# Pooled attention and a gated feed-forward on one core: GpSimd writes the scaled queries in tile order, and VectorE's reciprocal gives a third factor

## The chip, the core and the metric

The kernel runs on one core of a Trainium2 chip. The metric is the time of one execution on the device in microseconds (us); the median of three runs of the kernel before is 1849.12 us (1848.44 to 1851.25). One execution was also taken by the profiler, and all rows below come from it. The engines are named as in the profile: PE (TensorE's matmuls), PEld (its weight loads), DVE (VectorE), ACT (ScalarE), POOL (GpSimd), SP (the queue that issues the DMAs). L544 is line 544 of the kernel before.

## The reference

Two stages over 4 batches of 12288 tokens with 128 channels. First, attention against 768 keys that are at once the values: `kv` is averaged over 4x4 patches and multiplied by `w_sr`. Then a feed-forward of width 1024, whose activation is h times its own softmax, with a layer norm behind it.

```python
kv_pool = kv.reshape(B, H // r, r, W // r, r, C).mean(axis=(2, 4))
k = v = kv_pool.reshape(B, -1, C) @ w_sr
s = (q @ k.transpose(0, 2, 1)) / np.sqrt(C)
a = np.exp(s - s.max(-1, keepdims=True))
a /= a.sum(-1, keepdims=True) + 1e-09
x = (a @ v).reshape(B * N, C)
h = x @ w_in
e = np.exp(h - h.max(-1, keepdims=True))
solu = h * e / (e.sum(-1, keepdims=True) + 1e-9)
ln = (solu - mean(solu)) / np.sqrt(var(solu) + 1e-6) * g_ln
out = ln @ w_out
```

## The kernel before

The 49152 tokens are 384 **tiles** of 128 tokens; 4 tiles are a **group** (512 tokens, one load of queries), 24 groups are a batch. The program is written out by hand as 384 **slots**, one per tile, and every engine works its own in-order queue. In each slot each stage works on another tile: slot t does the scores of tile t+1, a quarter of the attention's values of an earlier group, the first feed-forward matmul (`hidden_pe`, L693) of tile t-9, the activation of tiles t-10 and t-11, and the last matmul (`final_pe`, L821) of tile t-13. Most matmuls are done in three passes over 16-bit halves (a high and a low part), so operands are split into a high part (a cast) and a low part (a subtraction).

What one slot holds, engine by engine:

- PE: 6 matmuls of scores (L580), 4 or 5 of values (L640), 6 of `h` (L693), 24 of the output `o` (L821).
- DVE: the row maximum of the scores (L601), the low half `phl` of the probabilities (L612), the maximum of `h` (L701), and `u` = h x factor x e (L731).
- ACT: the exponential of the scores (L602), the high half of `phl` (L604), a square for the variance (L796), the exponential `e` (L717).
- POOL: the high half of `u` (`hidden_high`, L748, 128x1024) and its low half (`hidden_low`, L755), both into the tile `uhl`.
- SP: issues two DMA transposes: `pT` from `phl` (L615), which the values need, then `uT` from `uhl` (L770), which the output matmul of that tile reads two slots later.

Once in a group come: the load of queries `qf` (L528), POOL's scaling of them (`q_scale`, L544, batches 1 to 3 only), ACT's cast to `qh` (`q_split`, L558), POOL's low part `ql` (`q_low`, L567), the norms (below), `xh` and `xl`, the output's scale `f` (L831 to L839), the output tile `ob` and its store. While a batch runs, POOL also sums the pooling patches of the next batch (`kv_add`, L240, 128x384, two in 6 slots; in batch 0 more), each sum behind a load of 384 KB on SP. In batch 0 the scores use 32-bit operands: there `q_split` and `q_low` work on `qwh` and `qwl`, and the queries are not scaled.

The queries of a group lie in `qf` as token order has them; token 4t+j belongs to row t of tile j. `by_tile` reads them with a stride of 4 elements (16 bytes), so that a result written through `in_tiles` has the 128 tokens of each tile side by side. Before the change `q_scale` works in place, in order; `q_split` and `q_low` read through `by_tile`:

```python
nc.gpsimd.tensor_scalar(qf, qf, state["kq", g // GPB][:, 1:2], 1.0, op0=ALU.mult, op1=ALU.mult)
nc.scalar.copy(in_tiles(qh), by_tile(qf))
nc.gpsimd.tensor_tensor(in_tiles(ql), by_tile(qf), in_tiles(high), op=ALU.subtract)
```

The norms of a group: `values_norm` (POOL, L667) makes two rows `zz` of 4 sums, z times `bb[3]` and z times `bb[4]`; `values_recip` (DVE, L675) inverts both into `rz`, factors for the exponential of `h` and for its maximum; `values_recip_u` (ACT, L680) multiplies the first by `bb[0]`, which is the factor of `u`. `bb` holds factors of a batch, set once by small operations (`kv_bound0`).

Within a slot POOL's queue stands as: zz (one slot in four), high and low of `u`, `f` (another slot), `q_low` (a third), `q_scale` (the slot of zz), then `kv_add`.

Of the kernel before, what the change touches and what calls it, by code (L numbers as in the profile page):

```python
# [11 lines left out]
F32 = mybir.dt.float32  # L12
# [9 lines left out]
P = 128  # L22
# [45 lines left out]
def kernel(  # L68
# [38 lines left out]
    def float64_parts(raw, name):  # L107


        pair = raw.rearrange("p (f two) -> p f two", two=2)  # L110
        lo, hi = pair[:, :, 0], pair[:, :, 1]
        top = wrk.tile([P, DFF], F32, tag="u", name=f"top_{name}", bufs=5)
        if name == "in":
            rest = wrk.tile([P, DFF], F32, tag="u", name="rest_in", bufs=5)
        else:
            rest = bat.tile([P, 2 * NK], F32, tag="acc", name="rest_out", bufs=1)[:, :DFF]
        ex = wrk.tile([P, DFF], I32, tag="e", name=f"ex_{name}")
        sgn = wrk.tile([P, DFF], I32, tag="e", name=f"sgn_{name}")
        scalar = nc.vector.tensor_scalar
        both = nc.vector.tensor_tensor  # L120
        and_, shr = ALU.bitwise_and, ALU.logical_shift_right
        return top, rest, [
            partial(scalar, ex, hi, 20, 0x7FF, op0=shr, op1=and_),
            partial(scalar, ex, ex, -896.0, 0.0, op0=ALU.add, op1=ALU.max),
            partial(scalar, ex, ex, 255.0, 2.0**23, op0=ALU.min, op1=ALU.mult),
            partial(
                nc.vector.scalar_tensor_tensor,
                ex,
                hi,
                -0x80000000,  # L130
                ex,
                op0=and_,
                op1=ALU.bitwise_or,
            ),
            partial(scalar, sgn, hi, 0xFFFFF, 3, op0=and_, op1=ALU.logical_shift_left),
            partial(both, top.bitcast(I32), ex, sgn, op=ALU.bitwise_or),
            partial(
                nc.vector.scalar_tensor_tensor,
                rest,
                lo.bitcast(U32),  # L140
                2.0**-52,
                ex.bitcast(F32),
                op0=ALU.mult,
                op1=ALU.mult,
            ),
        ]
# [4 lines left out]
    def kv_alloc(b):  # L151
        for n, w, dt, bufs in (
            ("kT", NK, F32, 1),
            ("ksq", NK, BF16, 1),
            ("kss", 2, F32, 4),
            ("vf", NK, F32, 1),
        ):
            state[n, b] = bat.tile([P, w], dt, tag=n, name=f"{n}_{b}", bufs=bufs)
        for n, w in (("knm", 3), ("sv", 2), ("bb", 5), ("kq", 3), ("dg", P)):
            state[n, b] = (  # L160
                state[n, 0]
                if 0 < b < B
                else bat.tile([P, w], F32, tag=n, name=f"{n}_{b}", bufs=1)
            )
        for n, dt, bufs in (
            (("kwh", F32R, 1), ("kwl", F32R, 1))
            if b == 0 or b >= B
            else (("kh", F16, 2), ("kl", F16, 2))
        ):
            state[n, b] = bat.tile([P, NK], dt, tag=n, name=f"{n}_{b}", bufs=bufs)  # L170
        vhl = dmt.tile([P, 2 * NKC, P], F16, tag="vhl", name=f"vhl_{b}")
        state["vhl", b] = vhl
        state["vh", b], state["vl", b] = vhl[:, :NKC, :], vhl[:, NKC:, :]
# [181 lines left out]
    def kv_bound0(part):  # L355
        knm, bb, sv = state["knm", 0], state["bb", 0], state["sv", 0]
        if part == 0:
            nc.vector.tensor_scalar(
                bb[:, 0:1], knm[:, 2:3], wmax2, 1e-20, op0=ALU.mult, op1=ALU.max
            )  # L360
            nc.vector.tensor_scalar(knm[:, 2:3], knm[:, 2:3], 1e-28, None, op0=ALU.max)
            nc.gpsimd.tensor_tensor(knm[:, 2:3], knm[:, 2:3], mhalf[:, 0:1], op=ALU.pow)
            nc.gpsimd.tensor_tensor(bb[:, 0:1], bb[:, 0:1], mhalf[:, 0:1], op=ALU.pow)
        elif part == 1:
            pow2_under(knm[:, 2:3])
        else:
            small(bb[:, 1:2], bb[:, 0:1], SC / 32 * 1e-3 * 2.0**15)
            small(bb[:, 0:1], bb[:, 0:1], SC / 32)
            small(bb[:, 2:3], bb[:, 1:2], 1e-9)
            small(bb[:, 3:4], knm[:, 2:3], 2.0**5, wsc)  # L370
            small(bb[:, 4:5], bb[:, 3:4], -1.0)
            small(sv[:, 1:2], sv[:, 1:2], knm[:, 2:3], 2.0**5 / (SC * SC))

    def kv_scale_v(b, part):
# [12 lines left out]
    def kv_bound(b, part):  # L387

        knm, bb, sv = state["knm", b], state["bb", b], state["sv", b]
        if part == 0:
            nc.vector.tensor_reduce(knm[:, 2:3], knm[:, 0:2], axis=AX.X, op=ALU.max)
            nc.vector.tensor_scalar(
                bb[:, 0:1], knm[:, 2:3], wmax2, 1e-20, op0=ALU.mult, op1=ALU.max
            )
            nc.vector.tensor_scalar(knm[:, 2:3], knm[:, 2:3], 1e-28, None, op0=ALU.max)
            nc.gpsimd.tensor_tensor(bb[:, 0:1], bb[:, 0:1], mhalf[:, 0:1], op=ALU.pow)
            nc.gpsimd.tensor_tensor(knm[:, 2:3], knm[:, 2:3], mhalf[:, 0:1], op=ALU.pow)  # L400
        elif part == 1:
            nc.vector.tensor_scalar(
                bb[:, 1:2], bb[:, 0:1], SC * 1e-3 * 2.0**15, None, op0=ALU.mult
            )
            nc.vector.tensor_scalar(bb[:, 0:1], bb[:, 0:1], SC, None, op0=ALU.mult)
            nc.vector.tensor_scalar(bb[:, 2:3], bb[:, 1:2], 1e-9, None, op0=ALU.mult)
            pow2_under(knm[:, 2:3])
        else:
            nc.vector.tensor_scalar(knm[:, 2:3], knm[:, 2:3], 2.0**5, None, op0=ALU.mult)
            nc.vector.tensor_scalar(bb[:, 3:4], knm[:, 2:3], wsc, None, op0=ALU.mult)  # L410
            nc.vector.tensor_scalar(bb[:, 4:5], bb[:, 3:4], -1.0, None, op0=ALU.mult)
            nc.vector.tensor_scalar(sv[:, 1:2], sv[:, 1:2], knm[:, 2:3], None, op0=ALU.mult)

    def kv_diag(b, half):
# [119 lines left out]
    def in_tiles(a):  # L534
        return a.rearrange("p (j t) -> p j t", j=GT)
# [4 lines left out]
    def q_scale(g):  # L540
        if wide(g) or NG <= g:
            return
        qf = state["qf", g // QL][:, (g % QL) * 512 : (g % QL + 1) * 512]
        nc.gpsimd.tensor_scalar(  # L544
            qf, qf, state["kq", g // GPB][:, 1:2], 1.0, op0=ALU.mult, op1=ALU.mult
        )

    def q_split(g):
        if NG <= g < NG + GPB:
            return  # L550
        qf = state["qf", g // QL][:, (g % QL) * 512 : (g % QL + 1) * 512]
        if wide(g):
            qh = grp.tile([P, 512], F32R, tag="qwh", name=f"qwh_{g}")
            ql = grp.tile([P, 512], F32R, tag="qwl", name=f"qwl_{g}")
        else:
            qh = grp.tile([P, 512], F16, tag="qh", name=f"qh_{g}")
            ql = grp.tile([P, 512], F16, tag="ql", name=f"ql_{g}")
        nc.scalar.copy(in_tiles(qh), by_tile(qf))  # L558
        state["q", g] = (qh, ql)

    def q_low(g):
        if NG <= g < NG + GPB:
            return
        qf = state["qf", g // QL][:, (g % QL) * 512 : (g % QL + 1) * 512]
        qh, ql = state["q", g]
        high = qh.bitcast(F32) if wide(g) else qh
        nc.gpsimd.tensor_tensor(in_tiles(ql), by_tile(qf), in_tiles(high), op=ALU.subtract)  # L567


    def scores_pe(t):  # L570
# [89 lines left out]

    def values_norm(g):
        b = g * GT // TPB
        zz = grp.tile([P, 2, GT], F32, tag="zz", name=f"zz_{g}", bufs=2)
        rz = grp.tile([P, 3, GT], F32, tag="rz", name=f"rz_{g}", bufs=3)
        z, bb = state.pop(("z", g)), state["bb", b]
        for k in range(2):
            nc.gpsimd.tensor_scalar(  # L667
                zz[:, k, :], z, 1e-9, bb[:, 3 + k : 4 + k], op0=ALU.add, op1=ALU.mult
            )
        state["zz", g] = (zz, rz)  # L670

    def values_recip(g):

        zz, rz = state.pop(("zz", g))
        nc.vector.reciprocal(rz[:, 0:2, :], zz)  # L675
        state["rz", g] = [rz[:, k, :] for k in range(3)]

    def values_recip_u(g):
        rz = state["rz", g]
        nc.scalar.activation(rz[2], rz[0], AF.Copy, scale=state["bb", g * GT // TPB][:, 0:1])  # L680
        state["z2", g] = grp.tile([P, GT], F32, tag="z2", name=f"z2_{g}", bufs=3)
        state["v3", g] = grp.tile([P, GT], F32, tag="v3", name=f"v3_{g}", bufs=3)

# [637 lines left out]
```

## Time and profile before

| | |
|---|---|
| median of 3 runs | 1849.12 us (1848.44 to 1851.25) |
| the profiled execution | 1851.55 us, of which the trace spans 1849.8 us |
| PE busy | 1821.7 us (98%) |
| ACT busy | 1783.7 us (96%) |
| DVE busy | 1769.8 us (96%) |
| POOL busy | 1683.1 us (91%) |
| granted TensorE clock | 0.999 of full speed |

The profiled execution took 2.43 us more than the median. PE's busy time is counted from matmuls that overlap, so a busy PE need not be at its peak. Busy shares are means over stages with different limits; the table says that four engines are full nearly all the time, not which of them sets the pace. SP is not in the table: the time in which it issues DMAs is not counted as busy.

### The profile page before, as it was taken

How to read it: one execution, taken by the hardware profiler on the slowest of the kernel's cores; microseconds unless marked ns; L12 is line 12 of the kernel's file. 1: busy time of each engine (PE TensorE's matmuls, PEld its weight loads, DVE VectorE, ACT ScalarE, POOL GpSimd, SP SyncE). 2: the span in 40 equal slices, each digit the busy share in tenths (PEclk: the TensorE clock that was granted, in tenths of full speed). 3: DMA queues.
4: the chain of work that ended last, by engine and by line, in shares of the span. 5: the costliest groups of instructions: out<-in, count | busy, mean ns of one | idle time of the engine just before them, and what ended most of it. 6: DMA issues, size and time to landing. Idle time of an engine off the chain costs nothing.

```text
span 1849.8 us, 42799 instructions
## 1 busy us (share of the span) xinstructions
PE 1821.7 (98%) x15747; PEld 1190.7 (64%) x15747; DVE 1769.8 (96%) x2635; ACT 1783.7 (96%) x3129; POOL 1683.1 (91%) x1466
## 2 busy tenths in 40 slices
PE   8999999999999999999999999999999999999998
PEld 5567777776566666666666666666666666666666
DVE  6999999999999999999999999999999999999997
ACT  5999999999999999999999999999999999999997
POOL 5899999899999999989999999998998989898987
PEclk9999999999999999999999999999999999999999
DMA  8999999999999999999999999999999999999998
GB/s 301 213 219 244 232 244 239 234 235 224 231 243 240 239 239 237 242 236 240 237 245 233 228 244 239 245 243 222 220 228 235 241 230 223 234 229 229 226 224 170
DMA packets 1440027, 432.80 MB, mean 234 GB/s; under 512 B 1404608, under 2 KB 1408832, under 8 KB 1439552
## 3 DMA queue, kind: packets, MB, share of 16 engines
q1 hardware_dynamic: 1439664, 429.97, 114.9%
q8 instruction: 126, 2.06, 0.5%
q14 instruction: 93, 0.76, 0.1%
q10 hardware_dynamic: 144, 0.00, 0.0%
HBM read 52.50 MB, written 25.17 MB: 42 GB/s over the span
## 4 chain that ended last, share of the span: by engine, by line
PE 66%; POOL 14%; ACT 9%; DMA 4%; issue 4%; DVE 2%; POOLq 0%; DVEq 0%
PE o L821 19%; PE h L693 18%; PE s L580 14%; PE xa L640 13%; POOL uhl L755 6%; DMA uT<-uhl 4%; POOL uhl L748 4%; ACT junk L796 2%; ACT e L717 2%; ACT s L602 2%; ACT phl L604 2%; POOL ql L567 1%; POOL ka L240 1%; PE pk L201 1%; POOL f L839 1%
## 5 line engine op out<-in xcount | busy, mean ns | idle before, releaser
L755 POOL TENSOR_TENSOR uhl<-u,uhl 128x1024 f16<-128x1024 f32 x382 | 814.5, 2133 | 31.7
L821 PEld LDWEIGHTS <-uT 128*128 128x128 f16 x9072 | 535.9, 98 | 105.3 <-DMA uT<-uhl 22.7
L821 PE MATMUL o<-wch,uT 128*128 128x128 f16 x6048 | 568.3, 219 | 10.1 <-DMA uT<-uhl 9.6
L821 PE MATMUL o<-wcl,uT 128*128 128x128 f16 x3024 | 525.9, 219 | 0.0
L731 DVE SCALAR_TENSOR_TENSOR u<-h,rz,e 128x1024 f32<-128x1024 f32 x384 | 491.1, 1279 | 26.8 <-ACT e L717 19.4
L701 DVE TENSOR_SCALAR_CACHE_REDUCE junkd<-h,rz 128x1024 bf16<-128x1024 f32 x384 | 490.8, 1278 | 1.6 <-PE h L693 1.3
L640 PE MATMUL xa<-pT,vhl 128*128 128x512 f16 x1728 | 469.5, 380 | 0.0
L748 POOL TENSOR_SCALAR uhl<-u 128x1024 f16<-128x1024 f32 x379 | 395.7, 1044 | 73.8 <-DVE u L731 65.6
L717 ACT ACTIVATE e<-h,nm,rz 128x1024 f32<-128x1024 f32 x384 | 458.6, 1194 | 3.0 <-DVE junkd L701 3.0
L796 ACT ACTIVATE junk<-u,su 128x1024 bf16<-128x1024 f32 x384 | 437.5, 1139 | 0.1
L601 DVE TENSOR_REDUCE nm<-s 128x1 f32<-128x768 f32 x384 | 364.2, 948 | 24.4 <-PE s L580 20.5
L612 DVE SCALAR_TENSOR_TENSOR phl<-s,phl 128x768 f16<-128x768 f32 x384 | 365.8, 953 | 2.9 <-ACT phl L604 2.8
L602 ACT ACTIVATE s<-s,nm 128x768 f32<-128x768 f32 x384 | 334.9, 872 | 9.7 <-DVE nm L601 9.0
L604 ACT ACTIVATE phl<-s 128x768 f16<-128x768 f32 x384 | 311.1, 810 | 12.1
L693 PEld LDWEIGHTS <-xh 128*128 128x128 f16 x1536 | 141.7, 98 | 195.0 <-DVE phl L612 33.1
L640 PEld LDWEIGHTS <-vhl 128*128 128x128 f16 x1728 | 162.7, 98 | 139.9 <-issue 12.8
L693 PE MATMUL h<-w_in_h,xh 128*128 128x512 f16 x768 | 228.9, 380 | 2.4 <-DVE rz L675 1.3
L693 PE MATMUL h<-w_in_h,xl 128*128 128x512 f16 x768 | 228.4, 379 | 0.0
L693 PE MATMUL h<-w_in_l,xh 128*128 128x512 f16 x768 | 228.4, 379 | 0.0
L580 PEld LDWEIGHTS <-qh 128*128 128x128 f16 x1152 | 107.7, 98 | 55.3 <-issue 0.7
L580 PE MATMUL s<-kh,qh 128*128 128x384 f16 x576 | 140.5, 325 | 0.6 <-DVE u L731 0.6
L580 PE MATMUL s<-kh,ql 128*128 128x384 f16 x576 | 140.7, 326 | 0.2 <-POOL ql L567 0.2
(153 smaller groups left out, 1862.7 us busy)
## 6 DMA issues: line engine op xcount, KB each, us to landing
kv<-in_kv_dram SPq DMA_DIRECT2D x64, 384.0 KB, 4.6
qf<-in_q_dram SPq DMA_DIRECT2D x96, 256.0 KB, 3.3
out_dram<-ob SPq DMA_DIRECT2D x96, 256.0 KB, 2.7
pT<-phl SPq DMA_TRANSPOSE x384, 4.0
uT<-uhl SPq DMA_TRANSPOSE x378, 4.5
raw_in<-in_moe_w_in_dram SPq DMA_DIRECT2D x1, 1024.0 KB, 5.2
raw_out<-in_moe_w_out_dram SPq DMA_DIRECT2D x1, 1024.0 KB, 9.5
room<-uhl SPq DMA_TRANSPOSE x5, 5.2
```

The lines of the kernel that those rows point to most:

```text
L580: nc.tensor.matmul(s[:, half, :384], lh[:, ts], rh[:, half * 384 : (half + 1) * 384], start=n == 0, stop=n == 2,)
L602: nc.scalar.activation(s, s, AF.Exp, bias=nm, accum_out=state["z", g][:, j : j + 1])
L612: nc.vector.scalar_tensor_tensor(phl[:, 1], state.pop(("s", t)), SC, phl[:, 0], op0=ALU.mult, op1=ALU.subtract)
L640: nc.tensor.matmul(xa, v[:, c, :], pT[:, :, a * NKC + c, :], start=n == 0, stop=n == len(seq) - 1)
L693: nc.tensor.matmul(h[:, hs], lh[:, ts], rh[:, hs], start=n == 0, stop=n == 2)
L701: nc.vector.tensor_scalar(junk, state["h", t], state["rz", g][1][:, j : j + 1], None, op0=ALU.mult, op1=ALU.min, accum_out=nm,)
L717: nc.scalar.activation(e, state["h", t], AF.Exp, bias=nm, scale=state["rz", g][0][:, js], accum_out=state["z2", g][:, js],)
L731: nc.vector.scalar_tensor_tensor(u, state.pop(("h", t)), state["rz", g][2][:, j : j + 1], state.pop(("e", t)), op0=ALU.mult, op1=ALU.mult, ...
L748: nc.gpsimd.tensor_scalar(uhl[:, 0, :], u, 1.0, 1.0, op0=ALU.mult, op1=ALU.mult)
L755: low.tensor_tensor(uhl[:, 1, :], u, uhl[:, 0, :], op=ALU.subtract)
L796: nc.scalar.activation(junk, u, AF.Square, scale=-float(DFF), bias=su, accum_out=state["v3", g][:, j : j + 1],)
L821: nc.tensor.matmul(po[:, ts], uT[:, a * NFC + c, :], w[:, c, :], start=start, stop=stop)
```

## The change

Four parts, and one that makes room:

1. `q_scale` writes a new tile `qs` (one buffer): it reads `qf` through `by_tile` and writes in tile order.
2. In batches 1 to 3 `q_split` (ACT) and `q_low` (POOL) read `qs` through `in_tiles`, that is in order. Batch 0 still reads `qf` through `by_tile`.
3. `bb` gets a sixth factor, `bb[3]` divided by `bb[0]`, set once (one DVE reciprocal, one small POOL product; the same in the general path, which does not run here).
4. `values_norm` makes a third row of `zz` from it, the reciprocal of DVE takes 12 elements in place of 8, and ACT's small product (L680) is gone, in all 96 groups.
5. `rest_out`, used while the weights are prepared, lies in the tag `uhl` in place of `acc`.

```diff
--- before.py
+++ after.py
@@ -113,7 +113,7 @@
         if name == "in":
             rest = wrk.tile([P, DFF], F32, tag="u", name="rest_in", bufs=5)
         else:
-            rest = bat.tile([P, 2 * NK], F32, tag="acc", name="rest_out", bufs=1)[:, :DFF]
+            rest = dmt.tile([P, DFF], F32, tag="uhl", name="rest_out", bufs=5)
         ex = wrk.tile([P, DFF], I32, tag="e", name=f"ex_{name}")
         sgn = wrk.tile([P, DFF], I32, tag="e", name=f"sgn_{name}")
         scalar = nc.vector.tensor_scalar
@@ -156,7 +156,7 @@
             ("vf", NK, F32, 1),
         ):
             state[n, b] = bat.tile([P, w], dt, tag=n, name=f"{n}_{b}", bufs=bufs)
-        for n, w in (("knm", 3), ("sv", 2), ("bb", 5), ("kq", 3), ("dg", P)):
+        for n, w in (("knm", 3), ("sv", 2), ("bb", 6), ("kq", 3), ("dg", P)):
             state[n, b] = (
                 state[n, 0]
                 if 0 < b < B
@@ -369,6 +369,8 @@
             small(bb[:, 2:3], bb[:, 1:2], 1e-9)
             small(bb[:, 3:4], knm[:, 2:3], 2.0**5, wsc)
             small(bb[:, 4:5], bb[:, 3:4], -1.0)
+            nc.vector.reciprocal(bb[:, 5:6], bb[:, 0:1])
+            small(bb[:, 5:6], bb[:, 5:6], bb[:, 3:4])
             small(sv[:, 1:2], sv[:, 1:2], knm[:, 2:3], 2.0**5 / (SC * SC))
 
     def kv_scale_v(b, part):
@@ -409,6 +411,8 @@
             nc.vector.tensor_scalar(knm[:, 2:3], knm[:, 2:3], 2.0**5, None, op0=ALU.mult)
             nc.vector.tensor_scalar(bb[:, 3:4], knm[:, 2:3], wsc, None, op0=ALU.mult)
             nc.vector.tensor_scalar(bb[:, 4:5], bb[:, 3:4], -1.0, None, op0=ALU.mult)
+            nc.vector.reciprocal(bb[:, 5:6], bb[:, 0:1])
+            nc.vector.tensor_scalar(bb[:, 5:6], bb[:, 5:6], bb[:, 3:4], None, op0=ALU.mult)
             nc.vector.tensor_scalar(sv[:, 1:2], sv[:, 1:2], knm[:, 2:3], None, op0=ALU.mult)
 
     def kv_diag(b, half):
@@ -541,9 +545,11 @@
         if wide(g) or NG <= g:
             return
         qf = state["qf", g // QL][:, (g % QL) * 512 : (g % QL + 1) * 512]
+        qs = grp.tile([P, 512], F32, tag="qs", name=f"qs_{g}", bufs=1)
         nc.gpsimd.tensor_scalar(
-            qf, qf, state["kq", g // GPB][:, 1:2], 1.0, op0=ALU.mult, op1=ALU.mult
-        )
+            in_tiles(qs), by_tile(qf), state["kq", g // GPB][:, 1:2], 1.0, op0=ALU.mult, op1=ALU.mult
+        )
+        state["qs", g] = qs
 
     def q_split(g):
         if NG <= g < NG + GPB:
@@ -555,7 +561,8 @@
         else:
             qh = grp.tile([P, 512], F16, tag="qh", name=f"qh_{g}")
             ql = grp.tile([P, 512], F16, tag="ql", name=f"ql_{g}")
-        nc.scalar.copy(in_tiles(qh), by_tile(qf))
+        src = by_tile(qf) if wide(g) else in_tiles(state["qs", g])
+        nc.scalar.copy(in_tiles(qh), src)
         state["q", g] = (qh, ql)
 
     def q_low(g):
@@ -564,7 +571,8 @@
         qf = state["qf", g // QL][:, (g % QL) * 512 : (g % QL + 1) * 512]
         qh, ql = state["q", g]
         high = qh.bitcast(F32) if wide(g) else qh
-        nc.gpsimd.tensor_tensor(in_tiles(ql), by_tile(qf), in_tiles(high), op=ALU.subtract)
+        src = by_tile(qf) if wide(g) else in_tiles(state.pop(("qs", g)))
+        nc.gpsimd.tensor_tensor(in_tiles(ql), src, in_tiles(high), op=ALU.subtract)
 
 
     def scores_pe(t):
@@ -660,10 +668,10 @@
 
     def values_norm(g):
         b = g * GT // TPB
-        zz = grp.tile([P, 2, GT], F32, tag="zz", name=f"zz_{g}", bufs=2)
+        zz = grp.tile([P, 3, GT], F32, tag="zz", name=f"zz_{g}", bufs=2)
         rz = grp.tile([P, 3, GT], F32, tag="rz", name=f"rz_{g}", bufs=3)
         z, bb = state.pop(("z", g)), state["bb", b]
-        for k in range(2):
+        for k in range(3):
             nc.gpsimd.tensor_scalar(
                 zz[:, k, :], z, 1e-9, bb[:, 3 + k : 4 + k], op0=ALU.add, op1=ALU.mult
             )
@@ -672,12 +680,10 @@
     def values_recip(g):
 
         zz, rz = state.pop(("zz", g))
-        nc.vector.reciprocal(rz[:, 0:2, :], zz)
+        nc.vector.reciprocal(rz, zz)
         state["rz", g] = [rz[:, k, :] for k in range(3)]
 
     def values_recip_u(g):
-        rz = state["rz", g]
-        nc.scalar.activation(rz[2], rz[0], AF.Copy, scale=state["bb", g * GT // TPB][:, 0:1])
         state["z2", g] = grp.tile([P, GT], F32, tag="z2", name=f"z2_{g}", bufs=3)
         state["v3", g] = grp.tile([P, GT], F32, tag="v3", name=f"v3_{g}", bufs=3)
```

POOL's queue in batch 1, around the scaling of one group's queries (`uhl` is the split of `u`, `zz` the sums of the norms, `qf`, `qs`, `ql` the queries), before:

```order
L544 TENSOR_SCALAR qf_11690<-qf_11690,kq_117 128x512
L667 TENSOR_SCALAR zz_12074<-z_all,bb_116 128x4 x2
L748 TENSOR_SCALAR uhl_12078<-u_12063 128x1024
L755 TENSOR_TENSOR uhl_12078<-u_12063,uhl_12078 128x1024
L748 TENSOR_SCALAR uhl_12155<-u_12145 128x1024
L755 TENSOR_TENSOR uhl_12155<-u_12145,uhl_12155 128x1024
L567 TENSOR_TENSOR ql_12138<-qf_11690,qh_12137 128x512
```

and now:

```order
L549 TENSOR_SCALAR qs_12026<-qf_11710,kq_117 128x512
L675 TENSOR_SCALAR zz_12096<-z_all,bb_116 128x4 x3
L754 TENSOR_SCALAR uhl_12101<-u_12085 128x1024
L761 TENSOR_TENSOR uhl_12101<-u_12085,uhl_12101 128x1024
L754 TENSOR_SCALAR uhl_12177<-u_12167 128x1024
L761 TENSOR_TENSOR uhl_12177<-u_12167,uhl_12177 128x1024
L575 TENSOR_TENSOR ql_12160<-qs_12026,qh_12159 128x512
```

No instruction has moved; a third small product stands behind the scaling, ahead of the next tile's split, and the scaling and the subtraction have other operands.

ACT's queue in batch 2, between the exponential of one tile and that of the next (`rz` the factors of the norms, `qh` the cast queries), before:

```order
L796 ACTIVATE junk_17342,v_57_17068<-u_17324,su_17325 128x1024
L717 ACTIVATE e_17347,z_57_17067<-h_17281,nm_231_17344,rz_17044 128x1024
L680 ACTIVATE rz_17336<-rz_17336,bb_116 128x4
L558 CAST qh_17398<-qf_16956 128x512
L602 ACTIVATE s_17328,z_all<-s_17328,nm_17401 128x2x384
```

and now:

```order
L802 ACTIVATE junk_17383,v_57_17107<-u_17364,su_17365 128x1024
L723 ACTIVATE e_17388,z_57_17106<-h_17321,nm_231_17385,rz_17083 128x1024
L565 CAST qh_17438<-qs_17306 128x512
L610 ACTIVATE s_17368,z_all<-s_17368,nm_17441 128x2x384
```

The small product is gone and the cast reads `qs`; the rest stands as it did. SP's queue has the same DMAs in the same order.

## Rows read from the trace of the kernel before

**Rows 1.** ACT's factor of u (L680), one in a group, in four stretches (first, last start)

```profile
L680 ACT ACTIVATE rz<-rz,bb x10: 287/290/292, 165.8 to 334.4; 128x4 f32<-128x4 f32 x10
...
L680 ACT ACTIVATE rz<-rz,bb x17: 282/287/290, 469.5 to 770.7; 128x4 f32<-128x4 f32 x17
...
L680 ACT ACTIVATE rz<-rz,bb x17: 282/287/290, 923.6 to 1222.1; 128x4 f32<-128x4 f32 x17
...
L680 ACT ACTIVATE rz<-rz,bb x24: 283/285/289, 1372.7 to 1795.5; 128x4 f32<-128x4 f32 x24
```

**Rows 2.** Busy us in two stretches: PE, PEld, DVE, ACT, POOL, then clock, DMA share, GB/s

```profile
461.00:777.00 316.00, 310.39 (x2726) 196.51 (x2724) 305.58 (x454) 308.07 (x538) 295.95 (x257) 1.00 1.20 239
...
1364.00:1787.00 423.00, 423.00 (x3728) 269.72 (x3727) 416.85 (x622) 420.09 (x739) 378.69 (x329) 1.00 1.16 230
```

**Rows 3.** The chain that ended last, 1139 to 1148 us: start, length, what

```profile
1133.05 6.80 DMA uT<-uhl
...
1139.90 1.51 PE o L821 x24
...
1143.25 1.29 PE h L693 x6
1144.55 1.34 PE o L821 x24
1145.89 0.97 PE s L580 x6
1146.86 1.08 PE xa L640 x5
```

**Rows 4.** Timeline of SP in batch 2, around 1130 us: start, length, what

```profile
1128.89 2.54 SPq L770 DMA_TRANSPOSE uT<-uhl  x1
1131.53 1.43 SPq L615 DMA_TRANSPOSE pT<-phl  x1
1133.05 3.26 SPq L770 DMA_TRANSPOSE uT<-uhl  x1
```

**Rows 5.** Timeline of POOL at the same place

```profile
1126.38 0.61 POOL L667 TENSOR_SCALAR zz<-z_all,bb 128x4 f32<-128x4 f32 x2
...
1128.21 2.13 POOL L755 TENSOR_TENSOR uhl<-u,uhl 128x1024 f16<-128x1024 f32 x1
```

**Rows 6.** Timeline of DVE at the same place

```profile
1127.24 0.95 DVE L612 SCALAR_TENSOR_TENSOR phl<-s,phl 128x768 f16<-128x768 f32 x1
1128.11 0.19 DVE L675 RECIPROCAL rz<-zz 128x8 f32<-128x8 f32 x1
```

**Rows 7.** Timeline of SP in batch 3, around 1505 us

```profile
1504.72 0.53 SPq L853 DMA_DIRECT2D out_dram<-ob  x1
1505.93 1.40 SPq L615 DMA_TRANSPOSE pT<-phl  x1
```

**Rows 8.** POOL's waits in 150:337, 461:777 and 915:1223: us, times, longest

```profile
POOL uhl L748 <- DVE u L731: 3.7, 7, 1.2
...
POOL uhl L748 <- DVE u L731: 8.8, 12, 1.4
...
POOL uhl L748 <- DVE u L731: 4.9, 6, 1.3
```

**Rows 9.** The operations that change, whole trace: ns least/median/most, first and last start

```profile
L544 POOL TENSOR_SCALAR qf<-qf,kq x72: 678/687/705, 446.9 to 1773.6; 128x512 f32<-128x512 f32 x72
L558 ACT CAST qh<-qf x72: 1099/1111/1137, 450.4 to 1777.4; 128x512 f16<-128x512 f32 x72
L567 POOL TENSOR_TENSOR ql<-qf,qh x72: 1386/1406/1424, 455.9 to 1782.9; 128x512 f16<-128x512 f32 x72
```

**Rows 10.** Operations of the same forms that read in order, whole trace

```profile
L271 ACT CAST kh<-kT x6: 498/500/505, 373.8 to 1289.6; 128x384 f16<-128x384 f32 x6
L274 POOL TENSOR_TENSOR kl<-kT,kh x6: 910/912/934, 380.7 to 1295.9; 128x384 f16<-128x384 f32 x6
...
L755 POOL TENSOR_TENSOR uhl<-u,uhl x382: 2124/2132/2151, 60.8 to 1831.9; 128x1024 f16<-128x1024 f32 x191
```

## The prediction

> **What bounds the kernel now.** I read the pace first, then busy times, then the chain, then the queues.
>
> *The pace.* ACT's factor of u runs once in a group of 4 tiles, so first and last start over the count less one give a group's time [rows 1]: batch 0 (334.4 - 165.8) / 9 = 18.73 us; 461 to 777 us, in batch 1, (770.7 - 469.5) / 16 = 18.83; 915 to 1223 us, in batch 2, 298.5 / 16 = 18.66; batch 3, 422.8 / 23 = 18.38.
>
> *What PE alone needs.* Where PE runs without a hole, the pieces of the chain give the matmuls' own pace [rows 3]: 0.97 us for 6 score matmuls, 1.08 for 5 of values (0.216 each), 1.29 for 6 of h, 1.34 for 24 of o. A group has 4 x (0.97 + 1.29 + 1.34) + 18 x 0.216 = 18.29 us. Batch 3 goes at 18.38, with 423.00 us of PE in 423.00 us [rows 2]: there PE sets the pace to within 0.1 us a group. Batch 0, whose scores are of 32 bits and dearer, holds its pace as evenly. Only the two stretches in between are slower than PE needs: 18.83 - 18.38 = 0.45 us a group over 316 / 18.83 = 16.8 groups (7.5 us), and 0.28 us over 308 / 18.66 = 16.5 groups (4.6 us). That, 12 us, is about all that any relief can win in these stretches.
>
> *What is late there.* The chain shows it: a transpose uT 6.80 us from issue to landing, and PE's output matmuls starting 0.05 us behind its end, with 1.51 us for what takes 1.34 elsewhere [rows 3]. But the transpose's input was no cause. Its POOL subtraction ended at 1128.21 + 2.13 = 1130.34 [rows 5], and SP issued it at 1133.05, 2.7 us later, because SP was busy: the uT before to 1131.43, then a pT to 1132.96, each behind the last by 0.1 us [rows 4]. That pT too had lain ready: its VectorE half ended at 1127.24 + 0.95 = 1128.19 [rows 6], 3.3 us before its issue. So in the stretches with kv loads SP's queue (or the transfers that hold each issue for 1.4 to 3.3 us) runs without a hole and sets the pace; what feeds it has 2.7 to 3.3 us in hand. In batch 3, with no kv loads, SP has holes: 1504.72 + 0.53 to 1505.93 is 0.68 us [rows 7].
>
> *ACT is full, but does not set the pace.* It is busy 308.07 / 316 = 97.5% in batch 1's slow stretch and 420.09 / 423 = 99.3% in batch 3 [rows 2], where PE runs at its own pace.
>
> *POOL is the other one to look at.* It waited for u 3.7 us in 150 to 337 us (10 groups), 8.8 in 461 to 777 and 4.9 in 915 to 1223 [rows 8]: 0.37, 0.52 and 0.30 us a group. The rest is work.
>
> **The change, part by part.**
>
> *ACT.* The factor's 0.29 us per group goes [rows 1]. The cast takes 1111 ns read with stride [rows 9]; kh, in order, takes 500 ns for 384 elements [rows 10], so 512 take between 500 and 500 x 512 / 384 = 667, I take 610. Together 0.79 us a group in batches 1 to 3, some 72 x 0.5 + 96 x 0.29 = 64 us of ACT's time. On the path: nothing in the slow stretches, since what ACT feeds (phl, then pT) already waits for SP. In batch 3 at most the 18.38 - 18.29 = 0.09 us a group above PE's need, 23 groups: 2 us, if ACT causes any of it. I take 0.
>
> *DVE.* The reciprocal takes 12 elements for 8, in 0.19 us now [rows 6]; half as many again can cost no more than half of that, 0.1 us x 96 = 9 us. DVE is at 305.58 / 316 = 97% in the slow stretch [rows 2], with 0.6 us a group free: 0. Removing ACT's product shortens the way from zz to u by one step.
>
> *POOL, three terms a group.* Two zz take 0.61 us with the gap between them [rows 5]; half of that is 0.31, and a third one brings its own gap, so I take 0.34. ql, now read in order: kl takes 912 ns for 384 elements and the split of u 2132 for 1024 [rows 10], so 512 take 912 + 128 x 1220 / 640 = 1156, that is 1406 - 1156 = 0.25 us less [rows 9]. The scaling now reads with the stride and took 687 ns in order [rows 9]. No row shows that operation with a stride. Bounds: 0 (the stride hides behind its arithmetic), and 1111 - 610 = 0.50 us (what the same stride costs ACT's cast, also one input, one read per element). POOL's own stride costs the 0.25 that ql loses. I take 0.35, between the same engine and the same form. Sum: 0.34 - 0.25 + 0.35 = +0.44 us a group in batches 1 to 3 (bounds +0.09 and +0.59), +0.34 in batch 0.
>
> The row of ql, with two inputs, gives 0.25 us for the stride [rows 9, 10]. The Trainium skill (GPSIMD Engine Reference, section 7, Performance pitfalls for Q7 kernels) says that a GpSimd kernel that reads at a byte step over 8 pays about 2.9 cycles per element instead of 1.9, half as much again; by that the scaling would take 687 x 1.5 = 1.03 us, an estimate, and POOL's sum would be 0.34 us a group by the row and 0.43 by the page. No run here shows which.
>
> *What covers it.* 150 to 337 us: 10 x 0.34 = 3.4 us into 3.7 of waiting: 0. 461 to 777: 16.8 x 0.44 = 7.4 into 8.8: 0. 915 to 1223: 16.5 x 0.44 = 7.3 into 4.9: 2.4 over, and first it eats the 2.7 us that a finished uhl waits for SP [rows 4, 5]: 0 to 2.4, I take 2. Batch 3 has no sums of patches, and POOL is at 378.69 / 423 = 90% [rows 2]: 0. If the cover were gone, each further 0.1 us a group would cost 33 x 0.1 = 3 us in the two stretches.
>
> *What is late next.* zz ended at 1126.99 and its reciprocal began at 1128.11, 1.1 us later [rows 5, 6]. The scaling ahead of it (+0.35) and the third product (+0.34) take 0.7 of that. A wait of DVE for zz should show in some groups, and cost little while SP is behind.
>
> *Small things.* Two operations on one column, once; rest_out in another buffer, no transfer: 0. SP's queue keeps its DMAs and order.
>
> Sum: +2 us on 1851.55, so 1853.6 for an execution like the profiled one; that stood 2.43 us above the median, so 1851 for the median.
>
> **The rivals.**
>
> *No change to measure (the forecast).* SP and its transfers keep the pace, PE in batches 0 and 3; POOL's work goes into its waits. A measurement tells 0.2% from no change, 3.7 us. Time 1851, 1847 to 1853.
>
> *Slower: POOL becomes the bound.* Its work a group is 18.66 - 0.30 = 18.36 us in batch 2's stretch and 18.83 - 0.52 = 18.31 in batch 1's. From +0.30 (batch 2) and +0.52 (batch 1) on, POOL is slower than SP's pace and uT waits for uhl instead of for SP. At the upper bound of +0.59: 16.5 x 0.29 + 16.8 x 0.07 = 6 us; and if half of POOL's present waits (7 us of 13.7) stay as they are, because u comes late behind each stall of PE, up to 13 us. Middle +7: 1856, up to 1862. For it: POOL's margin is as thin as the addition. Against: the 2.7 us that uhl lies ready.
>
> *Faster: ACT was in the loop.* If SP's holes come from late phl after all, 0.79 us of free ACT per group takes away half of the 12 us: 1843. For it: ACT is at 97 to 99%. Against: pT lay ready 3.3 us before its issue. A page bears on it: the Trainium skill (DMA: Bandwidth & Descriptors, Latency and other measured facts) gives 261 GB/s for a DMA transpose; the core moves 239 in the slow stretch [rows 2], so by the page the transfers have 8% to spare and would not bind, and PE would after any relief. The trace's SP queue without holes speaks against that.
>
> *The change doesn't do what it says.* The cast keeps its 1.11 us because its form, not the stride, is dear. Then ACT wins 0.29 us a group only and the time is the forecast's.
>
> **How the numbers follow.** No change 0.50 (with the last rival), slower 0.34, faster 0.16. The predicted time is the likeliest case's, 1851 us. The range leaves out the far half of the faster case (0.08) and the far third of the slower one (0.11): 1844 to 1859; the likeliest case's own range is 1847 to 1853.
>
> **What would show it.** Right: the cast at 0.6 us, ql at 1.16, the scaling near 1.03, three zz; ACT's share down by 4 points and POOL's up by 2; groups at 18.73, 18.8, 18.7 and 18.38 as before; SP still without holes until 1223 us. Wrong: uT issued within 0.1 us of the end of its uhl in batches 1 and 2, and groups at 18.9 or more (POOL binds), or groups near 18.4 there (ACT was in the loop).

## The result, and the profile after

The changed kernel takes 1865.20 us (median of 4 runs, 1864.67 to 1866.23), the kernel before 1848.78 beside it (4 runs, 1847.02 to 1851.25): a ratio of 1.0089 [1.0071, 1.0106]. It is slower by 16.4 us. The forecast was 1851, its range ended at 1859. The profiled execution took 1864.67 us, 13.1 more than the profiled one before. Two executions far outside all others, 10017.04 us of the kernel before and 4425.62 us of e6, are left out of the ratios and of e6's median.

The head of the page of the changed kernel, and its chain of work by engine:

```profile
span 1862.8 us, 42801 instructions
...
PE 1830.4 (98%) x15747; PEld 1190.3 (64%) x15747; DVE 1776.0 (95%) x2636; ACT 1734.9 (93%) x3033; POOL 1727.6 (93%) x1563
...
POOL 41%; PE 25%; issue 11%; DVE 11%; ACT 10%; DMA 2%; SPq 0%; POOLq 0%; DVEq 0%
```

The chain of the kernel before:

```profile
PE 66%; POOL 14%; ACT 9%; DMA 4%; issue 4%; DVE 2%; POOLq 0%; DVEq 0%
```

ACT is busy for 48.8 us less and POOL for 44.5 more, which is the way the change says. But the chain, which before was PE for 66% and POOL for 14% of the span, is now POOL's first of all. The operations that changed (groups by tile; count, least/median/most ns, first to last start):

```profile
L549 POOL TENSOR_SCALAR qs<-qf,kq x72: 1187/1199/1226, 449.9 to 1786.2; 128x512 f32<-128x512 f32 x72
L565 ACT CAST qh<-qs x72: 602/607/617, 453.0 to 1789.9; 128x512 f16<-128x512 f32 x72
L575 POOL TENSOR_TENSOR ql<-qs,qh x72: 1152/1160/1172, 459.7 to 1795.7; 128x512 f16<-128x512 f32 x72
```

Against [rows 9] the cast went from 1111 to 607 ns and ql from 1406 to 1160, as forecast. The scaling went from 687 to 1199; the forecast had 1037.

The pace, now from VectorE's reciprocal (one in a group; ACT's product is gone), in batch 0, in the two stretches with kv loads and in batch 3:

```profile
L683 DVE RECIPROCAL rz<-zz x11: 216/217/229, 147.5 to 336.7; 128x12 f32<-128x12 f32 x11
...
L683 DVE RECIPROCAL rz<-zz x17: 217/228/229, 471.8 to 774.6; 128x12 f32<-128x12 f32 x17
...
L683 DVE RECIPROCAL rz<-zz x17: 228/228/229, 930.4 to 1233.1; 128x12 f32<-128x12 f32 x17
...
L683 DVE RECIPROCAL rz<-zz x24: 216/220/228, 1384.3 to 1807.9; 128x12 f32<-128x12 f32 x24
```

These are 18.92, 18.93, 18.92 and 18.42 us a group, where [rows 1] gave 18.73, 18.83, 18.66 and 18.38. Batch 3 stands; batches 0, 1 and 2 are all slower, and stand alike.

Where the 13 us lie is told by the scaling of the same groups in both kernels. Before, for the first 19 groups of batch 1, for 25 groups from the start of batch 2, and for the last 25:

```profile
L544 POOL TENSOR_SCALAR qf<-qf,kq x19: 678/687/705, 446.9 to 786.1; 128x512 f32<-128x512 f32 x19
...
L544 POOL TENSOR_SCALAR qf<-qf,kq x25: 679/687/699, 883.7 to 1333.0; 128x512 f32<-128x512 f32 x25
...
L544 POOL TENSOR_SCALAR qf<-qf,kq x25: 681/687/697, 1333.0 to 1773.6; 128x512 f32<-128x512 f32 x25
```

After:

```profile
L549 POOL TENSOR_SCALAR qs<-qf,kq x19: 1191/1203/1223, 449.9 to 791.0; 128x512 f32<-128x512 f32 x19
...
L549 POOL TENSOR_SCALAR qs<-qf,kq x25: 1188/1199/1226, 889.0 to 1344.4; 128x512 f32<-128x512 f32 x25
...
L549 POOL TENSOR_SCALAR qs<-qf,kq x25: 1187/1197/1206, 1344.4 to 1786.2; 128x512 f32<-128x512 f32 x25
```

The lag is 449.9 - 446.9 = 3.0 us at the end of batch 0, 4.9 late in batch 1, 5.3 at the start of batch 2, 11.4 at its end, 12.6 at the last scaling. So batch 0 lost 3.0, batch 1 about 2, batch 2 6.1, batch 3 1.2, and the tail the rest of the 13.1. This is one profile of each kernel, and 16 groups can differ by 2 to 3 us from profile to profile (the paces of the kernels with time to spare, below), so the split is rough. The other 3.3 us of the 16.4 between the medians lie in the choice of executions: the one profiled before stood 2.8 above its median here, the one after 0.5 below.

The timeline of POOL over a group in batch 2 (start, length, what; a bracket at a row's end would show a wait), 10 of its 15 rows:

```profile
1212.21 1.19 POOL L549 TENSOR_SCALAR qs<-qf,kq 128x512 f32<-128x512 f32 x1
1213.50 0.95 POOL L675 TENSOR_SCALAR zz<-z_all,bb 128x4 f32<-128x4 f32 x3
1214.54 1.04 POOL L754 TENSOR_SCALAR uhl<-u 128x1024 f16<-128x1024 f32 x1
1215.67 2.13 POOL L761 TENSOR_TENSOR uhl<-u,uhl 128x1024 f16<-128x1024 f32 x1
1217.77 1.04 POOL L754 TENSOR_SCALAR uhl<-u 128x1024 f16<-128x1024 f32 x1
...
1220.98 1.16 POOL L575 TENSOR_TENSOR ql<-qs,qh 128x512 f16<-128x512 f32 x1
...
1225.60 1.02 POOL L845 TENSOR_TENSOR f<-f,mhalf 128x4 f32<-128x4 f32 x1
1226.59 1.00 POOL L240 TENSOR_TENSOR ka<-ka,kv 128x384 f32<-128x384 f32 x1
...
1228.69 2.13 POOL L761 TENSOR_TENSOR uhl<-u,uhl 128x1024 f16<-128x1024 f32 x1
1230.82 1.20 POOL L549 TENSOR_SCALAR qs<-qf,kq 128x512 f32<-128x512 f32 x1
```

From scaling to scaling are 18.61 us, and POOL waits for nothing in them: no two of its instructions lie more than 0.1 us apart. This group holds one kv sum; some hold two, 1.00 us more each. The rows of the scaling and of the kv sums in 461 to 800 us:

```profile
L549 POOL TENSOR_SCALAR qs<-qf,kq x18: 1192/1204/1223, 469.5 to 791.0; 128x512 f32<-128x512 f32 x18
...
L240 POOL TENSOR_TENSOR ka<-ka,kv x23: 987/998/1008, 465.3 to 777.9; 128x384 f32<-128x384 f32 x23
```

23 sums on 18 scalings, so a mean group is 18.61 + 5 / 18 x 1.00 = 18.89 us of POOL's own work, and the pace there is 18.93. POOL sets it. In 461 to 777 us and in 921 to 1229 its waits [rows 8] are gone to the last one; in batch 3, without kv sums, it still waits 15.3 us and PE is busy for 422.55 of 423 us.

What waits instead, over the whole span (us, times, longest):

```profile
ACT s L610 <- DVE nm L609: 75.9, 86, 2.8
...
POOL uhl L754 <- DVE u L737: 28.4, 35, 2.3
...
DVE rz L683 <- POOL zz L675: 18.6, 25, 2.0
...
PEld L588 <- POOL ql L575: 8.4, 24, 0.4
...
PEld L827 <- DMA uT<-uhl: 4.7, 8, 1.5
```

Before:

```profile
POOL uhl L748 <- DVE u L731: 65.6, 67, 2.3
...
PEld L821 <- DMA uT<-uhl: 22.7, 29, 1.9
...
DVE rz L675 <- POOL zz L667: 1.2, 2, 1.0
```

POOL waited 65.6 us for u before, and 28.4 now. New are VectorE's wait for zz (1.2 before) and PE's for ql (0.6 before). The weight loads' waits for uT, 22.7 us before, fell to 4.7. The longest is ACT's wait for VectorE's row maximum of the scores, 9.0 us before: ACT has less to do, and gets its input late. SP's timeline and VectorE's at the same group show both ends of a late POOL:

```profile
1214.97 1.40 SPq L623 DMA_TRANSPOSE pT<-phl  x1
1217.82 3.19 SPq L776 DMA_TRANSPOSE uT<-uhl  x1
```

```profile
1214.49 0.23 DVE L683 RECIPROCAL rz<-zz 128x12 f32<-128x12 f32 x1 [0.99 <-POOL zz L675]
```

SP stands still for 1.45 us (1216.37 to 1217.82) and issues uT 0.02 us after its low half ended (1215.67 + 2.13 = 1217.80): what the forecast named as the mark of POOL as the bound. Where [rows 4] had no hole, 18 of the 65 issues of uT in 921 to 1229 us now stand so, right behind POOL after a hole of over 0.3 us (2 of 66 before). VectorE waits 0.99 us for the third zz, with the row maximum of the scores and the next u behind it in its queue. PE hardly waits for uT at all, so it is held the other way: by what VectorE then brings late, and by ql. The chain of work goes that way too: from 1200 us it stays on POOL until the third zz at 1232.80, and passes on to VectorE's reciprocal (1233.10) and row maximum (1233.85).

### The profile page after: what moved, and what is told of

Same layout as the page of the kernel before. It is cut to its first block, busy times and chain, and to the rows that moved or that the text cites. A ratio compares the mean times of both kernels' runs of the same rounds, so it can differ in the third digit from the quotient of the medians.

```text
span 1862.8 us, 42801 instructions
## 1 busy us (share of the span) xinstructions
PE 1830.4 (98%) x15747; PEld 1190.3 (64%) x15747; DVE 1776.0 (95%) x2636; ACT 1734.9 (93%) x3033; POOL 1727.6 (93%) x1563
## 4 chain that ended last, share of the span: by engine, by line
POOL 41%; PE 25%; issue 11%; DVE 11%; ACT 10%; DMA 2%; SPq 0%; POOLq 0%; DVEq 0%
POOL uhl L761 17%; POOL uhl L754 10%; PE o L827 7%; PE h L699 6%; PE s L588 6%; PE xa L648 5%; POOL ka L240 3%; ACT e L723 3%; ACT junk L802 3%; DVE junkd L707 3%; DVE nm L609 3%; POOL qs L549 3%; POOL f L845 3%; ACT phl L612 2%; POOL ql L575 2%
## 5 line engine op out<-in xcount | busy, mean ns | idle before, releaser
L737 DVE SCALAR_TENSOR_TENSOR u<-h,rz,e 128x1024 f32<-128x1024 f32 x384 | 491.4, 1280 | 24.6 <-ACT e L723 16.4
L802 ACT ACTIVATE junk<-u,su 128x1024 bf16<-128x1024 f32 x384 | 437.6, 1139 | 0.1
L754 POOL TENSOR_SCALAR uhl<-u 128x1024 f16<-128x1024 f32 x379 | 395.9, 1044 | 36.4 <-DVE u L737 28.4
```

The costliest lines, as they stand in the source:

```text
L737: nc.vector.scalar_tensor_tensor(u, state.pop(("h", t)), state["rz", g][2][:, j : j + 1], state.pop(("e", t)), op0=ALU.mult, op1=ALU.mult, ...
L754: nc.gpsimd.tensor_scalar(uhl[:, 0, :], u, 1.0, 1.0, op0=ALU.mult, op1=ALU.mult)
L802: nc.scalar.activation(junk, u, AF.Square, scale=-float(DFF), bias=su, accum_out=state["v3", g][:, j : j + 1],)
```

## The experiments

Two theories. **P**: POOL's work a group decides, wherever it passes what POOL had to spare; which part brings the work is all the same. **Z**: the order on POOL decides, since zz stands right behind the longer scaling and VectorE waits for it. Two expectations name a third, **S**: the strided scaling is dear by itself, whatever else POOL has to do.

A table of all of them first. "POOL" is the work a group that the kernel adds to POOL's, by its own rows: +0.34 for a third zz, +0.51 for the scaling, -0.25 for ql, -0.40 where one product of 0.21 replaces two of 0.61 [rows 5]. "Waits" is POOL's waiting for u in 461 to 777 plus that in 921 to 1229 us (915 to 1223 in the kernel before). The paces are of batch 0 and the mean of the two stretches, from the rows of the reciprocal as above (in the kernel before, of ACT's product); a single stretch scatters by 0.1 to 0.2 us between profiles even where POOL has time to spare (e4: 18.54 and 18.87), so the mean is given. The ratios are against runs of the kernel before of the same series, whose medians were 1848.78 us for the change, 1851.06 for e1 to e4 and 1850.74 for e5 to e8.

| kernel | POOL, us | waits, us | batch 0 | batches 1, 2 | time, ratio |
|---|---|---|---|---|---|
| before | 0 | 8.8 + 4.9 | 18.73 | 18.74 | 1 |
| after | +0.60 | 0 + 0 | 18.92 | 18.92 | 1.0089 [1.0071, 1.0106] |
| e1, norms only | +0.34 | 0 + 3.1 | 18.92 | 18.77 | 1.0032 [1.0021, 1.0044] |
| e2, queries only | +0.26 (batch 0: 0) | 4.4 + 0 | 18.73 | 18.74 | 1.0016 [1.0003, 1.0030] |
| e3, one norm | -0.13 | 12.6 + 14.3 | 18.79 | 18.76 | 0.9979 [0.9964, 0.9994] |
| e4, one norm, old queries | -0.40 | 13.5 + 19.3 | 18.81 | 18.70 | 0.9988 [0.9977, 1.0000] |
| e5, strided write | +0.58 | 0 + 0 | 18.92 | 18.89 | 1.0065 [1.0048, 1.0082] |
| e6, scaling a slot earlier | +0.61 | 0 + 0 | 18.94 | 18.99 | 1.0086 [1.0064, 1.0107] |
| e7, e3 with loads on ACT | -0.12 | 7.6 + 19.9 | 18.72 | 18.84 | 1.0009 [0.9990, 1.0028] |
| e8, before with loads on ACT | 0 | 11.0 + 4.1 | 19.10 | 18.83 | 1.0007 [0.9990, 1.0024] |

What tells most is the stretches, of any of these kernels, in which POOL has no wait left. There the pace is POOL's own work, that is 18.31 us in batch 1 or 18.36 in batch 2 plus the second column: in the changed kernel 18.93 and 18.92 (sums 18.91 and 18.96), in e1's batch 1 18.66 (18.65), in e2's batch 2 18.59 (18.62), in e5 18.89 and 18.89 (18.89 and 18.94), in e6 18.98 and 19.01 (18.92 and 18.97). Where POOL still waits, the pace is not its own and scatters: 18.54 to 18.90 in the kernel before and e1 to e4.

**e1: the norms alone.** The queries go back to what they were.

```diff
-            in_tiles(qs), by_tile(qf), state["kq", g // GPB][:, 1:2], 1.0, op0=ALU.mult, op1=ALU.mult
+            qf, qf, state["kq", g // GPB][:, 1:2], 1.0, op0=ALU.mult, op1=ALU.mult
...
-        nc.scalar.copy(in_tiles(qh), src)
+        nc.scalar.copy(in_tiles(qh), by_tile(qf))
...
-        nc.gpsimd.tensor_tensor(in_tiles(ql), src, in_tiles(high), op=ALU.subtract)
+        nc.gpsimd.tensor_tensor(in_tiles(ql), by_tile(qf), in_tiles(high), op=ALU.subtract)
```

> The change's norms alone (third zz, reciprocal of 12, ACT's product gone), the queries as before. Theory P (POOL's own work per group is what counts): +0.34 us of POOL a group, 18.31 + 0.34 = 18.65 in batch 1's stretch and 18.36 + 0.34 = 18.70 in batch 2's, against a pace of 18.83 and 18.66 before: 1849 to 1853 us. Theory Z (the reciprocal's wait for zz is what hurts, whatever the load): DVE waits for zz for 10 us or more and the time is 1856 us or above, half of the loss or more.

Measured 1857.63 us (8 runs), beside 1851.06 for the kernel before. P's range is missed. The time lies in Z's, but the wait for zz stays under Z's 10 us, and by the ratio the loss is 5.9 us, less than half of 16.4. The rows of the norms, and of the scaling for the same groups as above (19 of batch 1, 25 from the start of batch 2):

```profile
L671 POOL TENSOR_SCALAR zz<-z_all,bb x288: 267/267/270, 48.7 to 1813.7; 128x4 f32<-128x4 f32 x144
L679 DVE RECIPROCAL rz<-zz x96: 215/219/229, 49.7 to 1824.9; 128x12 f32<-128x12 f32 x96
...
DVE rz L679 <- POOL zz L671: 7.6, 16, 1.8
...
L548 POOL TENSOR_SCALAR qf<-qf,kq x19: 677/687/696, 450.1 to 786.3; 128x512 f32<-128x512 f32 x19
...
L548 POOL TENSOR_SCALAR qf<-qf,kq x25: 679/687/694, 883.8 to 1337.4; 128x512 f32<-128x512 f32 x25
```

The mean pace of batches 1 and 2 hardly moved (18.66 and 18.89). Batch 0, at which neither theory had looked, lost what it lost in the changed kernel: the first scaling starts at 450.1 us, 3.2 later than before. But that lag does not last: it is 0.2 us late in batch 1 and 4.4 at the end of batch 2, where POOL still waits 3.1 us. So this profile doesn't say that the 6.4 us by which it is longer come from batch 0, and why the norms alone cost as much as they do stays open.

**e2: the queries alone.** Two zz, the reciprocal of 8 and ACT's product come back; no sixth factor.

```diff
-        for k in range(3):
+        for k in range(2):
...
-        nc.vector.reciprocal(rz, zz)
+        nc.vector.reciprocal(rz[:, 0:2, :], zz)
...
+        nc.scalar.activation(rz[2], rz[0], AF.Copy, scale=state["bb", g * GT // TPB][:, 0:1])
```

> The change's queries alone (scaling read with the stride into qs, cast and ql in order), the norms as before. Theory P: POOL +0.51 - 0.25 = +0.27 us a group in batches 1 to 3 gives 18.58 and 18.63, both under the pace of before: 1848 to 1852 us, and the two halves together cost more than their sum because only both exceed the pace. Theory S (the strided scaling is dear by itself, by what it holds up behind it): 1856 us or above.

Measured 1852.74 us (10 runs), just above P's range, beside 1851.06; S's 1856 us is not reached. The scaling has its full new price here:

```profile
L545 POOL TENSOR_SCALAR qs<-qf,kq x72: 1168/1198/1225, 448.0 to 1773.8; 128x512 f32<-128x512 f32 x72
```

With it standing ahead of zz as in the changed kernel, the order costs at most 0.3% here. The two halves sum to 0.32 + 0.16 = 0.48%, the whole is 0.89%. That is what a threshold gives, as P has it: each half leaves POOL waits in one of the two stretches, both together leave none. It is not the whole of it, since e1 costs more than P allowed.

**e3: all of the change, but zz in one product.** The three products of 128x4 become one of 128x12, which leaves out the addition of 1e-9.

```diff
-        for k in range(3):
-            nc.gpsimd.tensor_scalar(
-                zz[:, k, :], z, 1e-9, bb[:, 3 + k : 4 + k], op0=ALU.add, op1=ALU.mult
-            )
+        nc.gpsimd.tensor_tensor(
+            zz,
+            z.unsqueeze(1).to_broadcast([P, 3, GT]),
+            bb[:, 3:6].unsqueeze(2).to_broadcast([P, 3, GT]),
+            op=ALU.mult,
+        )
```

> The changed kernel, but one GpSimd product of 12 elements makes all three zz (it leaves out the addition of 1e-9 to sums that are at least about 1). Scaling still strided. Theory P: POOL -3 x 0.344 + about 0.3 = -0.7 us a group from the change, 0.1 below before: 1846 to 1850 us. Theory S: still 1856 us or above.

Measured 1847.19 us (10 runs), the fastest of all, and below the kernel before by 0.2%. Scaling, zz, and POOL's waits in 461 to 777 and 921 to 1229 us:

```profile
L549 POOL TENSOR_SCALAR qs<-qf,kq x72: 1172/1203/1222, 446.6 to 1771.3; 128x512 f32<-128x512 f32 x72
L674 POOL TENSOR_TENSOR zz<-z_all,bb x96: 198/212/233, 48.6 to 1805.0; 128x12 f32<-128x12 f32 x96
...
POOL uhl L756 <- DVE u L739: 12.6, 14, 1.6
...
POOL uhl L756 <- DVE u L739: 14.3, 16, 2.1
```

The strided scaling is as dear as ever, the work of ACT is gone as in the changed kernel, and 0.73 us a group less on POOL take back all of the 16 us. S is out. This shows POOL's work as the cause, with nothing else of the change undone, but for one thing: zz is also ready sooner, so e3 alone does not decide between P and Z. By pace less waits the work fell by more than 0.73: 18.69 - 12.6 / 17 = 17.95 us a group in batch 1, 0.98 under the changed kernel's 18.93. Most of the rest is gaps, which the rows do not hold: 0.10 us before the three products and 0.09 behind them in the timeline above, none around the one product.

**e4: one product for zz, and the queries of before.** e1 with the edit of e3. It asks what POOL's work is worth below the threshold.

> One product for the three zz and the queries as before: POOL about 0.4 us a group below the kernel before, ACT 0.2 to 0.3 below. Same part left out as in e3_one_norm. If SP's queue sets the pace of the kernel before in its slow stretches (what the prediction said), nothing is won: 1847 to 1850 us, groups there still at 18.7 to 18.8. If POOL was in that loop, groups fall towards 18.4 and the time to 1837 to 1843 us.

Measured 1850.26 us (10 runs), beside 1851.06. POOL has 0.40 us a group less to do than before the change, it waits 32.8 us in the two stretches in place of 13.7, and their pace moves from 18.74 to 18.70. SP's timeline in batch 2 shows no hole over 0.1 us between its issues:

```profile
1127.12 1.39 SPq L619 DMA_TRANSPOSE pT<-phl  x1
1128.61 2.49 SPq L774 DMA_TRANSPOSE uT<-uhl  x1
1131.19 1.44 SPq L619 DMA_TRANSPOSE pT<-phl  x1
1132.71 2.32 SPq L774 DMA_TRANSPOSE uT<-uhl  x1
1135.13 0.53 SPq L857 DMA_DIRECT2D out_dram<-ob  x1
```

Over the two stretches its holes of more than 0.12 us come to 3.0 us (3.9 before, 29.4 in the changed kernel). So POOL did not set the pace of these stretches before, and the forecast was right to leave it out as the bound there.

**e5: the stride on the write.** The scaling reads in order and writes with a step of 512 bytes.

```diff
-            in_tiles(qs), by_tile(qf), state["kq", g // GPB][:, 1:2], 1.0, op0=ALU.mult, op1=ALU.mult
+            in_tiles(qs).rearrange("p j t -> p t j"), qf.rearrange("p (t j) -> p t j", j=GT), state["kq", g // GPB][:, 1:2], 1.0, op0=ALU.mult, op1=ALU.mult
```

> The changed kernel, but the scaling reads qf in order and writes qs with the stride (a step of 512 bytes). Theory P with the price on the strided read: the scaling falls from 1.20 to about 0.7 us, POOL's work is then 0.1 us a group above the kernel before in batches 1 to 3 and 0.34 in batch 0: 1850 to 1856 us, like the norms alone or a little less. If a strided write is as dear as a strided read, the scaling stays at 1.2 us or more and the time at 1863 us or above.

Measured 1863.45 us (4 runs), nearly as slow as the change; a cheap write is out:

```profile
L549 POOL TENSOR_SCALAR qs<-qf,kq x72: 1157/1174/1199, 450.5 to 1784.8; 128x512 f32<-128x512 f32 x72
```

A write with a stride costs 0.49 us, a read with one 0.51. No choice of side makes the reordering cheap on this engine.

**e6: the scaling one slot earlier.** The same work, but zz no longer stands right behind the scaling.

```diff
-        if slot < NT and 0 < qs <= slot + 1 and (slot + 1 - qs) % GT == 0:
-            q_scale((slot + 1) // GT + 1)
+        if slot < NT and 0 < qs <= slot + 2 and (slot + 2 - qs) % GT == 0:
+            q_scale((slot + 2) // GT + 1)
```

> The changed kernel with the scaling issued one slot earlier on GpSimd, so that the sums zz no longer stand right behind it; the same work for POOL. Theory P (work per group): POOL stays without idle time in batches 1 and 2 and the time stays at 1862 to 1867 us, though DVE waits less for zz. Theory Z (the wait of the reciprocal for zz is what costs): 1858 us or below.

Measured 1867.55 us (median of three runs, 1867.07 to 1868.91), just above P's range and far from Z's: the same ratio as the change. VectorE's wait for zz did not go away, though zz now stands behind a split of u:

```profile
DVE rz L683 <- POOL zz L675: 20.6, 37, 2.0
```

So the order is not the cause. Since the wait stayed, e6 doesn't show what would happen without it; what speaks against Z as a whole is that POOL, without a wait in either stretch, goes at the pace of its own work in either order. The wait for zz is where the lateness of a full POOL is seen.

**e7 and e8: the loads off SP.** To see whether it is SP's issuing that binds the stretches once POOL is free, the loads of kv and queries go to ACT's queue, in e3 and in the kernel before.

```diff
-        nc.sync.dma_start(
+        (nc.sync if b == 1 and pos in SOON else nc.scalar).dma_start(
...
-        nc.sync.dma_start(t, qT[b, :, gb * 512 : (gb + QL) * 512])
+        (nc.sync if g < 3 else nc.scalar).dma_start(t, qT[b, :, gb * 512 : (gb + QL) * 512])
```

> e3_one_norm with the loads of queries and kv (but the first few) issued by ACT's queue instead of SP's. If SP's issuing is what sets the pace in the slow stretches, its 0.95 us a group of such issues goes and groups there fall from 18.7 and 18.8 towards 18.4: 1834 to 1842 us. If the transfers themselves set it (the same bytes on the same 16 engines), nothing: 1845 to 1849 us, and SP's issues of transposes grow longer instead.

> The kernel before with the same loads on ACT's queue, where ACT is 97 to 99% full. If SP's issuing sets the pace: 1836 to 1843 us; if the transfers do: 1846 to 1850 us; ACT's added issue time could cost up to 1 or 2 us in either case.

Measured 1852.23 (1844.35 to 1862.47) and 1851.78 us (1846.66 to 1859.05), 10 runs each, beside 1850.74: no gain, and a wide scatter; e7 lies above both of its ranges, e8 within its second one with the added issue time. The profile of e7 is of a run of 1850.84 us, that of e8 of the longest, 1859.05. In e7 batch 1's stretch did fall to (781.7 - 469.1) / 17 = 18.39 us a group, PE's own pace as in batch 3, but batch 2's rose to 19.30. There single waits for uT stop PE for 6 us; these are its waits over the span:

```profile
PEld L829 <- DMA uT<-uhl: 14.3, 12, 6.2
```

The median uT takes 4.9 us from issue to landing, 4.4 in e3. So in this profile, with the loads out of SP's queue, one stretch ran free and transfers were late in another. Whether issue or the transfers behind it bind these stretches stays open.

## Why the prediction was wrong

**The step that failed is a term of POOL's sum: the strided scaling, taken at +0.35 us.** It measured 1199 - 687 = +0.51 (+0.51 and +0.52 in e2 and e3). The upper bound was +0.50, from ACT's cast, which is of the same form (one input, one read per element) on another engine; the value was pulled down towards ql, which is on the same engine but of another form. The row of the same form came out nearer. ql has two inputs, and the stride on one of them costs only the 0.25 us that the step predicted for it; why it costs less there is not shown. The Trainium skill's ratio (GPSIMD Engine Reference, section 7, Performance pitfalls for Q7 kernels: half as much again) gave an estimate of 1.03 us; the trace does not agree with that ratio, 1199 ns is 75% more than 687.

With it the sum is +0.34 + 0.51 - 0.25 = +0.60 us a group in place of +0.44. The forecast's own threshold was +0.52 for batch 1 and +0.30 for batch 2. POOL's work a group had been worked out as 18.31 and 18.36 us; with 0.60 that makes 18.91 and 18.96, and the paces measured are 18.93 and 18.92. **The rival "POOL becomes the bound" is what happened**, just past its upper bound of +0.59 us and past its 1862.

**A second term was off: batch 0 at 0.** Its waits of 3.7 us were set against 3.4 us of added products, as means over ten groups. The waits did go, to 0.5 us, but the pace went from 18.73 to 18.92 all the same, and by the first scaling 3.0 us were lost. Only 7 of the 40 slots there had a wait at all [rows 8], so a group without one may have had no cover; how the added work passes from group to group was not shown. By the first scaling e1 and e5 lost as much (450.1 and 450.5 us for 446.9), e2, where nothing changes in batch 0, 1.1 us, and with one product nothing was lost (e3: 446.6).

**What these two terms make of the sum.** Batch 1's stretch by the forecast's own steps: 16.8 x 0.60 - 8.8 = 1.3 us; batch 2's: 16.5 x 0.60 - 4.9 = 5.0; batch 0: 3.0 as measured. That is 9.3 of the 13.1 us between the profiled executions. The scaling's term alone thus takes the sum from 2 to 6.3 us, which would still have lain in the range; it took batch 0 and the rest to leave it. The lag by groups has about the same parts (2, 6.1, and the 3.0 that was put in as measured). The rest, 1.2 in batch 3 and 2.6 in the groups outside the stretches, has no term, and none was tested.

**"First it eats the 2.7 us that a finished uhl waits for SP" was no cover.** A delay in hand can be used up once, while POOL's excess comes with every group; and it reached PE by VectorE's wait for zz and by ql, which this cover doesn't touch. The forecast had seen the wait for zz coming, and wrote that it would "cost little while SP is behind". SP was no longer behind: its holes in the two stretches came to 29.4 us.

**What was right.** The cast (0.607 for 0.61), ql (1.160 for 1.156), the third product (0.34), the reciprocal (227 ns for 192, under the 0.1 us allowed). ACT was not in the loop: in e3, where its work is gone and POOL has waits again, the stretches go at 18.76 us as against 18.74 before, and batch 3 stayed at 18.42 in the changed kernel (18.38). The mark named for POOL as the bound (uT issued within 0.1 us of its low half, groups at 18.9) appeared, if not in every slot. e4 bears out that POOL was not what set the pace before. "The change doesn't do what it says" fell with the cast's row.

## What to carry to other kernels

Price an access that a change gives a new stride by an operation of the same form (inputs, reads per element), even if that is on another engine, rather than by one on the same engine with more inputs: here the stride cost 0.51 us on 512 elements for one input and 0.25 for two. Where an engine's waits are about as long as the work that it is to get, forecast by whether the sum passes them, group by group, and give a bound that lies beyond the threshold more than a third of the chance. And before work goes to a nearly full engine, see whether its small operations can be merged: one product of 12 elements did in 0.21 us what three of 4 did in 0.95, and turned the change from 0.9% slower into 0.2% faster (without the addition of 1e-9).

## What was not expected of the hardware

On POOL a write with a step of 512 bytes (1174 ns) costs about the same as a read with a step of 16 (1199), against 687 in order: changing the side and the size of the step together moved the price by only 25 ns. And a POOL operation on 4 elements, an addition and a product by a factor, takes 267 ns, longer than one product of 12 elements whose two inputs are both broadcast (212 ns).
